# A recurrent attention kernel whose groups are brought one stage closer together, with three transposes moved to another engine

## The chip, the cores and the metric

One core of one Trainium2 chip. Times are device microseconds of one execution.

## The reference

```python
for t in range(S):                              # q, k, v, alpha: (4, 8, 768, 48)
    state = alpha[:, :, t, :, None] * state + einsum('bhd,bhe->bhde', k[:, :, t], v[:, :, t])
    y[:, :, t] = einsum('bhd,bhde->bhe', q[:, :, t], state)
x = y.transpose(0, 2, 1, 3).reshape(B, S, H * D)          # (4, 768, 384)
proj = x @ w_in                                           # 384 -> 1024
val, gate = proj[..., :512], proj[..., 512:]
for t in range(S):
    h = exp(A_log)[0] * h + val[:, t]                     # a[0, 0], as the reference has it
    ys[:, t] = h
out = (silu(gate) * ys) @ w_out                           # 512 -> 384
```

`w_in` and `w_out` come as float64 and are converted on the chip, in 12 units.

## The kernel before

The sequence is cut into N = 12 groups of 256 steps (4 batches of NG = 3 groups). A group goes through three stages, each a generator that the schedule steps: `front` (q, k and alpha are turned so that channels lie on the partitions; the running products V and P of alpha are scanned; Q = q·P, K = k·V; scores; keys turned back), `back` (states, values, eviction to `x_sb`, and `features`, which turns `x_sb` into `xT`), and `ssm` (four chunks of 6 matmuls, each chunk followed by a scan `hh`, a SiLU and a product `f`; then two output halves). In the profiles each of these matmuls counts as two instructions, so a chunk is 12 there (576 `pj` for 12 groups of four chunks). Each engine runs its instructions in the order in which the schedule issues them, as the profiles show: in the kernel before, the transposes for K end on TensorE at 210.13 us (209.09 + 1.04), but VectorE, which has `f` ahead of K, waits 0.45 us for the SiLU, starts `f` at 210.43 and K at 210.77.

```python
def load_heads(dst, src, n, queue=nc.sync):
    b, g = divmod(n, NG)
    for c in range(G):
        rows = ds(g * GC + c * C, C)
        queue.dma_start(out=dst[:, c, :, 0:D], in_=src[b, :, rows, :].rearrange("h p d -> p h d"))

def ssm(n, xT, prev_h, pool, ps_mm):
    ...
    for cc in range(NI):
        pj = ps_mm.tile([C, 2, GC], FP32, tag="mm", name="pj")
        ...                                      # 6 matmuls of w_in against xT (12 in the trace)
        nc.vector.tensor_tensor_scan(out=hh, ...)
        nc.scalar.activation(sg, pj[:, 1, :], AF.Silu)
        nc.vector.tensor_mul(f[:, cc, :], sg, hh)
        yield
    for c in range(G):
        ...                                      # output half: 4 matmuls of w_out (8 in the trace), eviction, store
        yield

def features(x_sb, xT, ps_tp):
    for c in range(G):
        ...                                      # 3 transposes on TensorE
        nc.scalar.activation(xT[:, :, ds(c * C, C)], tp, AF.Copy)

def front(n):
    ...
    def turned(name, jj):                        # 4 transposes on TensorE into PSUM (2 buffers)
        ...
    for jj in range(NP // 2):
        tp = turned("a", jj)
        ...                                      # scans V, reciprocal, scans P
    yield
    ...                                          # Q from turned("q", jj) and P; yield
    ...                                          # K from turned("k", jj) and V; yield
    ...                                          # scores, masked; yield
    keys_back(K, Kn, ps_tp)
    yield

for n in range(N + 3):                           # turn n: front(n), back(n-1), ssm(n-2), outputs of n-3
    ...
```

So a group's `xT` is finished in one turn and multiplied by `w_in` only in the next. While the weights are still being converted (turns 0 to 2), the conversion of units is placed between the steps.

## Time and profile before

| kernel | median us | range | profiled span | TensorE busy | VectorE busy |
|---|---|---|---|---|---|
| before | 347.33 (4 runs) | 346.2 to 348.6 | 344.2 | 309.7 | 198.6 |

The time of a run exceeds its own span (first to last instruction of the profile) by 1.6 to 2.3 us; the profiled run of this kernel took 345.98 us.

Cut at 98.1 us, where its steady turns have begun, and at the end of the turn of group 11 (295.9 us), this kernel is a start of 98.1, eight turns of together 197.8 (TensorE busy for 197.8), and an ending of 48.3 us.

### The profile page before, as it was taken

How to read it: one execution, taken by the hardware profiler on the slowest of the kernel's cores; microseconds unless marked ns; L12 is line 12 of the kernel's file. 1: busy time of each engine (PE TensorE's matmuls, PEld its weight loads, DVE VectorE, ACT ScalarE, POOL GpSimd, SP SyncE). 2: the span in 40 equal slices, each digit the busy share in tenths (PEclk: the TensorE clock that was granted, in tenths of full speed). 3: DMA queues.
4: the chain of work that ended last, by engine and by line, in shares of the span. 5: the costliest groups of instructions: out<-in, count | busy, mean ns of one | idle time of the engine just before them, and what ended most of it. 6: DMA issues, size and time to landing. Idle time of an engine off the chain costs nothing.

```text
span 344.2 us, 9637 instructions
## 1 busy us (share of the span) xinstructions
PE 309.7 (90%) x4233; PEld 249.6 (73%) x4233; DVE 198.6 (58%) x374; ACT 126.5 (37%) x267; POOL 32.3 (9%) x54
## 2 busy tenths in 40 slices
PE   2556696879999999999999999999999999997994
PEld 1345585757877878868868878878878878776772
DVE  2869797683566566475484494484475574314140
ACT  1356876743324324324333342333233233222111
POOL 4023652440000000000000000000000000000000
PEclk9996798989999999999999999999999999999998
DMA  9999998504704907608609409519110010010101
GB/s 129 216 218 256 238 199 125 94 2 103 130 2 97 135 2 130 104 0 146 88 1 160 73 2 170 62 38 170 29 46 4 0 48 2 2 49 0 50 0 54
DMA packets 107650, 29.02 MB, mean 84 GB/s; under 512 B 100944, under 2 KB 107088, under 8 KB 107600
## 3 DMA queue, kind: packets, MB, share of 16 engines
q1 hardware_dynamic: 104992, 27.93, 46.4%
q10 hardware_dynamic: 2608, 0.40, 1.0%
q8 instruction: 35, 0.57, 0.7%
q14 instruction: 15, 0.12, 0.1%
HBM read 23.60 MB, written 4.72 MB: 82 GB/s over the span
## 4 chain that ended last, share of the span: by engine, by line
PE 80%; DVE 8%; ACT 5%; DMA 3%; issue 2%; SPq 1%; ACTq 0%; DVEq 0%
PE pj L93 36%; PE o L107 18%; PE tp L295 9%; PE z L131 3%; PE sc L332 3%; PE y L146 3%; PE y L164 3%; PE tpk L119 3%; PE tpx L173 2%; DVE V L302 2%; DVE P L307 2%; DMA a_pad<-in_alpha_dram 2%; DMA v_sb<-in_v_dram 1%; ACT ex L242 1%; ACT ex L241 1%
## 5 line engine op out<-in xcount | busy, mean ns | idle before, releaser
L93 PE MATMUL pj<-xT,w_in 128*128 128x256 f32 x576 | 135.2, 386 | 2.9 <-ACT sg L101 2.9
L93 PEld LDWEIGHTS pj<-xT,w_in 128*128 128x128 f32 x576 | 107.1, 192 | 17.5 <-POOL w_out L250 3.0
L107 PE MATMUL o<-w_out,f 128*128 128x384 f32 x192 | 65.9, 496 | 0.1
L96 DVE TENSOR_TENSOR_SCAN hh<-a_dec,hh,pj 128x256 f32<-128x256 f32 x32 | 23.9, 747 | 69.0 <-PE pj L93 69.0
L101 ACT ACTIVATE sg<-pj 128x256 f32<-128x256 f32 x48 | 18.4, 383 | 114.1 <-DVE hh L96 114.0
L107 PEld LDWEIGHTS o<-w_out,f 128*128 128x128 f32 x192 | 35.9, 192 | 23.7 <-DVE f L102 0.7
L102 DVE TENSOR_TENSOR f<-sg,hh 128x256 f32<-128x256 f32 x48 | 20.9, 436 | 25.4 <-ACT sg L101 25.4
L302 DVE TENSOR_TENSOR_SCAN V<-tp,bias 128x256 f32<-128x256 f32 x48 | 30.1, 669 | 6.9 <-PE tp L295 6.9
L307 DVE TENSOR_TENSOR_SCAN P<-tp,iV,bias 128x256 f32<-128x256 f32 x48 | 33.4, 737 | 0.8
L312 ACT ACTIVATE junk<-V,bias 128x1024 f32<-128x1024 f32 x12 | 13.8, 1148 | 47.2 <-DVE V L302 47.2
L295 PE MATMUL tp<-ident,a_pad 128*128 128x128 f32 x96 | 13.9, 289 | 14.0 <-POOL k_pad L201 4.9
L96 DVE TENSOR_TENSOR_SCAN hh<-a_dec,pj 128x256 f32<-128x256 f32 x16 | 11.0, 685 | 23.8 <-PE pj L93 23.8
L295 PEld LDWEIGHTS tp<-ident,a_pad 128*128 128x128 f32 x96 | 11.6, 147 | 15.9 <-POOL k_pad L201 4.9
L349 POOL TENSOR_TENSOR S_n<-S_end,V 128x192 f32<-128x192 f32 x7 | 3.6, 513 | 203.5 <-DVE S_end L358 203.5
L295 PE MATMUL tp<-ident,q_pad 128*128 128x128 f32 x96 | 14.4, 292 | 8.0 <-DVE P L307 6.4
L295 PEld LDWEIGHTS tp<-ident,q_pad 128*128 128x128 f32 x96 | 11.9, 151 | 12.2 <-issue 8.6
L335 DVE COPY_PREDICATED A<-mask,sc 128x512 f32<-128x512 uint8 x24 | 16.0, 720 | 3.0 <-PE sc L332 3.0
L319 DVE TENSOR_TENSOR Q<-tp,P 128x512 f32<-128x512 f32 x24 | 15.4, 681 | 2.9 <-PE tp L295 2.9
L332 PEld LDWEIGHTS sc<-Q,K 64*64 64x64 f32 x768 | 13.7, 143 | 4.0 <-issue 3.0
L110 ACT ACTIVATE o_sb<-o 128x384 f32<-128x384 f32 x24 | 10.7, 479 | 15.5 <-PE o L107 15.5
L323 DVE TENSOR_TENSOR K<-tp,V 128x512 f32<-128x512 f32 x24 | 15.5, 681 | 0.5 <-PE tp L295 0.5
L332 PE MATMUL sc<-Q,K 64*64 64x64 f32 x768 | 15.5, 231 | 0.1
(61 smaller groups left out, 313.8 us busy)
## 6 DMA issues: line engine op xcount, KB each, us to landing
a_pad<-in_alpha_dram SPq DMA_DIRECT2D x24, 192.0 KB, 4.7
k_pad<-in_k_dram SPq DMA_DIRECT2D x24, 192.0 KB, 5.2
v_sb<-in_v_dram SPq DMA_DIRECT2D x24, 192.0 KB, 5.1
out_dram<-o_sb SPq DMA_DIRECT2D x24, 192.0 KB, 2.2
q_pad<-in_q_dram SPq DMA_DIRECT2D x22, 192.0 KB, 4.9
bits<-in_moe_w_in_dram SPq DMA_DIRECT2D x8, 384.0 KB, 5.3
bits<-in_moe_w_out_dram SPq DMA_DIRECT2D x4, 384.0 KB, 5.1
q_pad<-in_q_dram ACTq DMA_DIRECT2D x2, 192.0 KB, 5.5
```

The costliest lines, as they stand in the source:

```text
L93: nc.tensor.matmul(pj[:, i, :], w_in[:, kk, i, ds(cc * C, C)], xT[:, kk, :], start=(kk == 0), stop=(kk == NK - 1))
L96: nc.vector.tensor_tensor_scan(out=hh, data0=a_dec[:, cc:cc + 1].to_broadcast([C, GC]), data1=pj[:, 0, :], initial=prev_h[cc][:, GC - 1:GC ...
L101: nc.scalar.activation(sg, pj[:, 1, :], AF.Silu)
L102: nc.vector.tensor_mul(f[:, cc, :], sg, hh)
L107: nc.tensor.matmul(o, f[:, cc, ds(c * C, C)], w_out[:, cc, :], start=(cc == 0), stop=(cc == NI - 1))
L295: nc.tensor.transpose(tp[:, u, ds(c * C, C)], pad[name][:, c, 2 * j:2 * j + 2, :], ident)
L302: nc.vector.tensor_tensor_scan(out=V[:, 2 * jj + u, GC - 1::-1], data0=tp[:, u, ::-1], data1=bias[:, 1:2].to_broadcast([C, GC]), initial=1 ...
L307: nc.vector.tensor_tensor_scan(out=P[:, 2 * jj + u, :], data0=tp[:, u, :], data1=bias[:, 1:2].to_broadcast([C, GC]), initial=iV0[:, 2 * jj ...
L319: nc.vector.tensor_mul(Q[:, js], turned("q", jj), P[:, js])
L323: nc.vector.tensor_mul(K[:, js], turned("k", jj), V[:, js, 1:GC + 1])
L332: nc.tensor.matmul(scv[ds(R * r, R), i, c * NP + j, :], K[rows, j, steps], Q[rows, j, steps], start=True, stop=True, skip_group_check=True)
L335: nc.vector.copy_predicated(out=A[:, i].rearrange("p x t -> p (x t)"), mask=mask[:, ds(i * GP * R, GP * R)], data=sc[:, i])
```

## The change

Intent: a group's SSM block follows it one turn sooner (group n - 1 instead of n - 2), and from the fifth group on the q, k and alpha transposes are VectorE's, so TensorE gets 24 transposes less in each of eight groups. The loads of these groups place blocks of 32x32 for VectorE's transpose (`W = 32` in the kernel); they come in batches of a whole sequence, in packets of 128 and 64 bytes. Conversion of a unit is cut in two (U: split, J: join) and placed inside the first SSM blocks. The schedule becomes a string per turn: F a step of front(n), A of front(n+1), B of back(n), S of ssm(n-1), O an output of n-2, L and M loads.

```diff
+        BY_VECTOR = NG + 1
+        def load_batch(b):
+            ...
+                for j, nj in [(0, NP)] if w0 == 0 else [(j, 1) for j in range(NP)]:
+                    for i in range(2):
+                        for half in range(2):
+                            ...
+                            nc.sync.dma_start(out=tv[ds(DP * i + W * half, W), ...], in_=src[...])
         def front(n):
+            def squares(name, dst):
+                nc.vector.transpose(dst, batches[b, name][:, :, ds(g * GC, GC)])
+            if by_vector:
+                squares("a", aT)
             for jj in range(NP // 2):
-                tp = turned("a", jj)
+                tp = aT[:, js] if by_vector else turned("a", jj)
                 ...                              # scans V, P of half jj
+                yield
+            if by_vector:
+                squares("q", Q)
-                nc.vector.tensor_mul(Q[:, js], turned("q", jj), P[:, js])
+                nc.vector.tensor_mul(Q[:, js], Q[:, js] if by_vector else turned("q", jj), P[:, js])
             ...                                  # the same for k, K, V
-            nc.sync.dma_start(out=out[...], in_=o_sb)
+            nc.scalar.dma_start(out=out[...], in_=o_sb)
-        places = {0: (0, 0, 0, 1, 1), 1: (1, 1, 1, 1, 2), 2: (1, 1, 1, 1, 1)}
+        early = ["FFFFLUFUJFBJBBB", "FUUSJJFUUSJJFUUSJJFLSFFBUBJUBJB", "FUSJUFJSFFFFOBBSABASABOM"]
+        usual = "FLSSFFOABBSABASBOM"
+        ending = ["SSOSOS", "OO"]
-            for n in range(N + 3):
+            for n in range(N + 2):
                 ...
```

(Cut: heads are paired differently, tiles share memory, buffers of Q, K, A, Kn and x_sb are one fewer, the fallback path follows suit.)

## The prediction

> **What bounds the kernel now.** I read the page's busy times and its strip of 40 slices first, then the busy time by stretches (one per turn), then the groups, then the three timelines of one steady turn.
>
> ```profile
> PE 309.7 (90%) x4233; PEld 249.6 (73%) x4233; DVE 198.6 (58%) x374; ACT 126.5 (37%) x267; POOL 32.3 (9%) x54
> PE   2556696879999999999999999999999999997994
> DMA  9999998504704907608609409519110010010101
> ...
> 0.00:20.00 20.00, 8.98 (x96) 6.82 (x96) 11.00 (x18) 4.53 (x7) 4.04 (x23) 1.00 1.27 171
> 20.00:45.00 25.00, 15.07 (x339) 12.87 (x342) 21.34 (x43) 19.86 (x40) 12.46 (x12) 0.80 1.10 252
> 45.00:73.00 28.00, 21.24 (x311) 17.64 (x306) 21.68 (x44) 19.39 (x39) 11.58 (x13) 0.93 0.77 107
> 98.10:122.83 24.73, 24.73 (x344) 20.16 (x343) 15.10 (x28) 8.26 (x18) 0.52 (x1) 1.00 0.49 82
> ```
>
> The reader sees two kernels in one. From 73 us on a turn takes 24.73 us and TensorE is busy for all of it; nothing else is near full (VectorE 15.1). Nine such turns (groups 3 to 11) run from 73 to 296 us, then some 48 us of last SSM work. Before 73 us TensorE is idle for about 28 us, at a granted clock down to 0.80, and VectorE (21.3 of 25) and ScalarE (19.9 of 25) carry the load: this is where the weights are converted.
>
> ```profile
> L295 PE MATMUL tp<-ident,a_pad 128*128 128x128 f32 x96 | 13.9, 289 | 14.0 <-POOL k_pad L201 4.9 <-ACT Kn L120 4.1 <-issue 3.1
> L101 ACT ACTIVATE sg<-pj 128x256 f32<-128x256 f32 x48 | 18.4, 383 | 114.1 <-DVE hh L96 114.0
> L102 DVE TENSOR_TENSOR f<-sg,hh 128x256 f32<-128x256 f32 x48 | 20.9, 436 | 25.4 <-ACT sg L101 25.4
> ...
> 206.39 2.86 PE L93 MATMUL pj<-xT,w_in 128*128 128x256 f32 x12
> 209.29 0.69 DVE L96 TENSOR_TENSOR_SCAN hh<-a_dec,pj 128x256 f32<-128x256 f32 x1 [2.16 <-PE pj L93]
> 210.01 0.39 ACT L101 ACTIVATE sg<-pj 128x256 f32<-128x256 f32 x1 [3.31 <-DVE hh L96]
> 210.43 0.43 DVE L102 TENSOR_TENSOR f<-sg,hh 128x256 f32<-128x256 f32 x1 [0.45 <-ACT sg L101]
> 210.77 1.28 DVE L323 TENSOR_TENSOR K<-tp,V 128x512 f32<-128x512 f32 x2
> ...
> 206.77 2.28 SPq L83 DMA_DIRECT2D a_pad<-in_alpha_dram  x2
> ```
>
> These lines give the latency of an SSM chunk: hh starts 0.2 us after the last of its 12 matmuls, the SiLU waits for hh, f waits for the SiLU; from the start of hh to the next VectorE instruction is 1.48 us, 0.45 of it idle. VectorE and ScalarE run in program order, so each such wait also holds all behind it. The last line shows that the issue of two 1024-packet loads holds its queue for 2.28 us.
>
> [...] 104992 packets took 46.4% of 16 engines' 344.2 us, 24 ns each, though most hold only 192 B. [...]
>
> **Part 1, transposes off TensorE.** In the steady turn the q, k and alpha transposes hold TensorE 0.96 + 0.97 + 0.96 = 2.9 us (from start to start of the next group, for example 105.41 to 106.37). Eight of twelve groups lose them: 23 us of TensorE work gone, and a TensorE-bound turn would be 24.7 - 2.9 = 21.9 us. VectorE gains three transposes[...]: V/P scans 5.6, hh 2.8, f 1.4, A 1.3, states 1.5, Q and K 2.6[...], SiLU waits 1.8, in all 20.4 of 21.9 us. That fits only if nothing waits.
>
> **Part 2, the new turn's loop.** The stages are now one turn closer, so I followed the program order with measured durations, from the start of the last hh of a turn (t = 0). SiLU ends at 1.1. ScalarE then evicts xT (0.87), because features come after that chunk in its order: 2.0. TensorE's next chunk needs this xT: start 2.2. From there TensorE is full: two chunks 5.3, scores 1.1, key transposes 0.9, half an output 2.6, states 1.1, values 1.1, third chunk 2.7, to 17.0. Then hh, SiLU, f 0.2 + 1.5, V/P scans of the next group's second half 2.8, [...]Q multiply 1.3, and the last hh can start: 23.9 us. In that time TensorE has 21.9 us of work; the 2.0 us between are idle after the last output. So I expect about 23.9 us a turn, 0.8 less than now, not 2.9. ScalarE now also issues two v loads and two output stores, before the junk pair (2.5 us) and the first SiLU. Up to about 1.4 us per load this is hidden by the wait for the second chunk; at 2.4 us, as in a crowded queue, the turn becomes about 26.
>
> **Part 3, the start.** Converting one unit costs ScalarE 2.2, VectorE 0.7 + 0.5, GpSimd 2.0 us. Six w_in units now stand inside the first SSM block: each chunk needs the two units before it joined, and its SiLU stands behind the ScalarE work of the two units after. From f to f: two joins 1.0, V/P 2.8, first mask 0.35, ScalarE 1.75 + 0.55 + 1.75, SiLU and f 0.85: 9.0 us. The other two chunks go through join, GpSimd 3, matmuls 2.9, hh to f 1.5: 8.5. Group 0 passes front and back alone, about 34 us until its xT (alpha lands at 7.5; the old trace has K at 17.8, and conversions, Kn, states, values and evictions add 16). First f 8.7 later, three more chunks 26, then A to xT of group 1 11.5: 80 us. The next turn (two groups' V/P, one SSM block, VectorE-bound with ScalarE's waits) adds 32: the turn of group 3 starts at 112, or 115 with matmuls at the lowered clock[...] in the old trace. The old kernel is at the like point (SSM of group 1 multiplied) at 98. So the shorter pipeline does not shorten the start; I expect it to lose some 15 us there.
>
> **Sum.** Start 115 + eight turns with a following group 8 x 23.9 = 191 + turn of group 11, TensorE-bound, 21.9 + last SSM block and outputs 16.1 + 5.3 + flag and f waits 3.5 + tail 4.8 = 357.6 us of span. Run time is 347.34 - 344.2 = 3.1 us above the span: 361. This charges every wait I can see. If half of the start's loss is absent (106) and the turn is 22.7 us, the same sum gives 106 + 181.6 + 51.6 + 3.1 = 342. Hand chains of this length tend to double-count, and such a carefully arranged schedule was presumably meant to gain, so I take the middle, **350 us**.
>
> **Rivals.** (a) TensorE stays the bound: turn 21.9, start as good as before in useful work (103): 103 + 175.2 + 51.6 + 3.1 = 333 us. For it: 20.4 of 21.9 us on VectorE does fit. Against it: the loop from hh through SiLU, xT and the next chunk has no slack. (b) ScalarE's issues hold the first SiLU: 25 to 26 us a turn, 8 x 1.5 more, some 370 us. For it: 2.3 to 4.8 us per pair of loads in the SP rows; against: only while the queue is crowded. (c) The loads bind. 8 groups x 3 tensors x 2048 more packets = 49152, at 20 to 24 ns over 16 engines 61 to 74 us more transfer time, on 160 us in a span of 350: room on average, but a batch of three groups takes some 46 us. It is asked for two turns ahead, so I think it is hidden; late by one tensor it costs 5 to 15 us once.
>
> **Range and chances.** 334 to 364 us: from rival (a) to the full sum. Faster by over 2% (below 340.4) needs both a good start and a TensorE-bound turn: 0.25. Within 2%: 0.43. Slower (above 354.3): 0.32.
>
> **What would show it.** Steps are right if steady turns measure 23 to 25 us with TensorE idle 1 to 3 us, ended by the xT eviction or a SiLU, while VectorE is above 80% busy; if the first steady turn starts after 108 us[...]. Wrong if turns are 22 us without idle TensorE[...], if the start is over by 100, or if TensorE waits for the new batch loads.

Cut, where marked, are reasons, with the duration of a VectorE transpose: an estimate that no trace had shown, as the kernel before has no such instruction. The sums still contain it: three such terms in the 20.4 us of VectorE a turn, one in the loop's 23.9 us, and so eight in 191, in the 357.6 us of span and in the 361 us of time. The terms that can still be read come to 17.0 and 22.8 us. The 24 ns per packet is the profile page's average; from 80 to 93 us the same trace has 19.4 ns (8605 packets, 80.3% of 16 engines' 13 us).

## More of the kernel before

Beside the lines that the prediction shows, one more matters, the chain of work that ended last, followed back from the last instruction, as shares of the span by engine:

```profile
PE 80%; DVE 8%; ACT 5%; DMA 3%; issue 2%; SPq 1%; ACTq 0%; DVEq 0%
```

TensorE (PE) is four fifths of the chain.

## The result, and the profile after

The changed kernel takes **364.6 us** (4 runs, 363.01 to 365.35), against 347.33 before: ratio 1.049 [1.044, 1.054], slower.

Busy times, the strip of TensorE in 40 slices, and the chain by engine, from the page of the changed kernel:

```profile
PE 296.5 (82%) x4041; PEld 232.3 (64%) x4041; DVE 230.8 (64%) x397; ACT 127.2 (35%) x267; POOL 57.3 (16%) x72
...
PE   2558276684895997998998989979989799799993
...
PE 57%; DVE 24%; ACT 8%; DMA 4%; issue 3%; POOL 1%; SPq 1%; DVEq 0%; POOLq 0%; ACTq 0%
```

TensorE is busy for 13 us less (not 23: the group of `pj` matmuls alone, the same 576, takes 141.7 us instead of 135.2, part of them at a lower clock: the mean granted over the span is 0.941, against 0.973) and for a smaller share of a longer span: after the start its slices now read 7, 8 and 9, where the old kernel had a row of nines. In the chain VectorE's share has gone from 8% to 24%. The same, by stretches (columns: length; busy time of TensorE, its weight loads, VectorE, ScalarE, GpSimd, each with its count; granted clock; DMA share; GB/s). The stretches are the turns of groups 1 and 2, then two steady turns:

```profile
32.69:77.28 44.59, 26.86 (x344) 21.54 (x344) 26.83 (x53) 24.96 (x50) 17.00 (x16) 0.81 0.46 99
77.28:119.56 42.28, 32.25 (x379) 25.74 (x379) 25.73 (x46) 12.31 (x26) 12.70 (x11) 0.85 0.28 39
...
192.80:216.81 24.01, 22.03 (x318) 17.26 (x318) 19.37 (x32) 8.16 (x19) 0.51 (x1) 1.00 1.14 116
264.46:288.48 24.02, 22.04 (x319) 17.27 (x319) 18.98 (x32) 8.17 (x19) 0.51 (x1) 1.00 0.15 35
```

Cut in three like the old kernel:

| | start | eight turns | ending | span |
|---|---|---|---|---|
| before | 98.10 | 197.80 | 48.30 | 344.2 |
| after | 119.56 | 192.79 | 48.55 | 360.9 |
| difference | +21.46 | -5.01 | +0.25 | +16.7 |

The eight turns gained 5 us, not the 23 us that the removed transposes had held TensorE; the start lost 21. (The start ends where the turn of group 4 begins in the old kernel and that of group 3 in the changed one, with the SSM of group 1 multiplied in both. The two do not stand at exactly the same instruction, so this is an accounting, not yet an explanation.)

The chain in one steady turn, in order of time (start, us, what), shows why it takes 24 us:

```profile
190.91 0.67 DVE hh L105
...
191.88 0.88 ACT xT L183 x2
...
192.80 5.45 PE pj L102 x24
...
204.96 2.80 PE pj L102 x12
...
207.78 0.76 DVE hh L105
...
209.41 1.20 DVE V L338 x2
...
210.82 1.64 DVE P L343 x2
212.46 1.15 DVE Q L329
...
213.63 1.29 DVE Q L352 x2
214.92 0.67 DVE hh L105
...
215.89 0.88 ACT xT L183 x2
...
216.81 1.35 PE pj L102 x5
```

It is a closed loop: from the `hh` of one turn's last chunk (190.91) through the xT eviction and TensorE's work to the next turn's (214.92), 24.01 us. The old chain at this place is TensorE alone. VectorE's leg in it, 207.78 to 214.92, is scans, the new q transpose (L329, 1.15) and a multiply, all of them ahead of `hh` in VectorE's order. TensorE's wait at the seam, from the view of waits (total, times, longest):

```profile
PE pj L102 <- ACT xT L183: 14.6, 8, 2.0
PE pj L102 <- POOL w_in L288: 12.4, 4, 6.8
PE tp L325 <- DVE P L343: 7.8, 3, 4.0
```

The first line is the loop: eight waits, 1.8 us each. The other two are the start: chunks that wait for converted weights, and TensorE transposes that wait for a scan to free one of the two PSUM buffers they write into.

### The profile page after: what moved, and what is told of

Its sections match the earlier page's. It is cut to its first block, busy times and chain, and to the rows that moved or that the text cites. A ratio compares the mean times of both kernels' runs of the same rounds, so it can differ in the third digit from the quotient of the medians.

```text
span 360.9 us, 9309 instructions
## 1 busy us (share of the span) xinstructions
PE 296.5 (82%) x4041; PEld 232.3 (64%) x4041; DVE 230.8 (64%) x397; ACT 127.2 (35%) x267; POOL 57.3 (16%) x72
## 4 chain that ended last, share of the span: by engine, by line
PE 57%; DVE 24%; ACT 8%; DMA 4%; issue 3%; POOL 1%; SPq 1%; DVEq 0%; POOLq 0%; ACTq 0%
PE pj L102 28%; PE o L116 12%; DVE P L343 5%; DVE V L338 5%; DVE hh L105 4%; PE sc L372 4%; PE z L140 3%; DVE Q L352 3%; PE tpk L128 3%; PE y L155 3%; DVE Q L329 3%; PE tp L325 2%; ACT xT L183 2%; DMA batch<-in_k_dram 2%; ACT sg L110 2%
## 5 line engine op out<-in xcount | busy, mean ns | idle before, releaser
L102 PE MATMUL pj<-xT,w_in 128*128 128x256 f32 x576 | 141.7, 401 | 27.0 <-ACT xT L183 14.6
L110 ACT ACTIVATE sg<-pj 128x256 f32<-128x256 f32 x48 | 18.2, 380 | 115.6 <-DVE hh L105 115.5
L325 PE MATMUL tp<-ident,pads 128*128 128x128 f32 x96 | 18.5, 339 | 19.5 <-DVE P L343 7.8
L228 POOL MEMSET batch<- 32x1536 f32 x18 | 24.7, 1371 | 53.3 <-DMA batch<-in_q_dram 31.8
L325 PEld LDWEIGHTS tp<-ident,pads 128*128 128x128 f32 x96 | 14.1, 172 | 23.5 <-issue 14.5
L343 DVE TENSOR_TENSOR_SCAN P<-aT,iV,bias 128x256 f32<-128x256 f32 x32 | 23.4, 773 | 0.6
L338 DVE TENSOR_TENSOR_SCAN V<-aT,bias 128x256 f32<-128x256 f32 x32 | 20.6, 685 | 0.3
L360 ACT ACTIVATE junk<-V,bias 128x1024 uint8<-128x1024 f32 x12 | 13.8, 1147 | 18.3 <-issue 14.1
L338 DVE TENSOR_TENSOR_SCAN V<-tp,bias 128x256 f32<-128x256 f32 x16 | 10.1, 672 | 15.7 <-PE tp L325 15.7
L140 PE MATMUL z<-v_sb,Kn 64*64 64x48 f32 x768 | 13.8, 220 | 4.5 <-ACT Kn L129 4.5
L173 PEld LDWEIGHTS y<-S_n,Q 64*64 64x64 f32 x704 | 13.1, 140 | 6.4 <-ACT fence L160 3.3
L173 PE MATMUL y<-S_n,Q 64*64 64x48 f32 x704 | 14.6, 227 | 3.0 <-ACT fence L160 3.0
```

Source lines behind the costliest of these rows:

```text
L102: nc.tensor.matmul(pj[:, i, :], w_in[:, kk, i, ds(cc * C, C)], xT[:, kk, :], start=(kk == 0), stop=(kk == NK - 1))
L140: nc.tensor.matmul(zv[chs, r, g, j, :], Kn[rows, g, j, chs], v_sb[rows, g, NP * i + j, :], start=True, stop=True, skip_group_check=True)
L173: nc.tensor.matmul(yv[at, i, c, j, :], Q[rows, j, ds(R * x, R)], S_n[rows, x, j, :], start=False, stop=(c == G - 1 and j == NP - 1), skip_ ...
L228: nc.gpsimd.memset(tv[ds(DP * i + W, W), :, D - W:W], 1.0 if name == "a" else 0.0)
L325: nc.tensor.transpose(tp[:, u, ds(c * C, C)], pad[name][:, c, j], ident)
L338: nc.vector.tensor_tensor_scan(out=V[:, 2 * jj + u, GC - 1::-1], data0=tp[:, u, ::-1], data1=bias[:, 1:2].to_broadcast([C, GC]), initial=1 ...
```

## The experiments

Each is an edit of the changed kernel unless said otherwise; "before" ran in the same rounds. All results were correct but one, which is named.

### 1. e1_swap: the last SSM chunk before the next group's q

```diff
-        usual = "FLSSFFOABBSABASBOM"
+        usual = "FLSSFFOABBSABSBAOM"
```

The same instructions; only the last S and B (SSM chunk, features) now stand before the A that holds the q transpose and Q.

> Edit: in the steady turn the last SSM chunk's scan, SiLU and product stand ahead of the next group's q transpose and Q multiply, instead of behind them. Theory (the loop hh, SiLU, xT, two chunks ... third chunk, V/P, q transpose, Q, hh sets the turn): the loop loses 2.4 us and drops to 21.5, below TensorE's 21.9 to 22.0 us of work, so the turns of groups 3 to 10 go from 23.8 to 24.0 to about 22.0, TensorE no longer waits for xT, and the run goes from 364 to about 349 us. Rival (ScalarE's v loads, stores and junk pair hold the first SiLU): the turn stays within 0.3 us of 23.9, the run above 361. Rival (VectorE is simply full): the turn stays too, as no VectorE work is taken away.

Measured: 345.77 us (344.85 to 347.53), ratio to before 0.9996 [0.9956, 1.0036]; span 342.7, so 18.2 us under the changed kernel's. The first two of its eight turns take 22.6 and 22.2 us, the other six 21.8; all eight 175.41 (119.34 to 294.75), against 192.79. Two of the six by stretches:

```profile
185.88:207.64 21.76, 21.76 (x319) 17.36 (x318) 18.63 (x32) 8.28 (x18) 0.51 (x1) 1.00 1.15 121
207.64:229.42 21.78, 21.78 (x335) 17.37 (x334) 18.70 (x32) 8.48 (x18) 0.51 (x1) 1.00 1.14 118
```

TensorE is busy for all of a turn of 21.8 us, with VectorE's load what it was (18.6 us) and the DMA share the same 1.15. So the 2 us a turn came from the place of the q work in VectorE's order, not from VectorE's total or the batch loads. This kernel, 3 us better than expected, only equals the old one because its start (119.34) is still as long as the changed kernel's.

### 2. e2_start: the first SSM block joins its units in another order

```diff
-  early[1] = "FUUSJJFUUSJJFUUSJJFLSFFBUBJUBJB"
+  early[1] = "UUFJJSUUFJJSUUFJJSFLSFFBBBBUUJJ"
```

The two units of a chunk are joined one step sooner, ahead of the scan and SiLU of the chunk before; two w_out units go to the end of the turn.

> Edit: only the order of the turn of group 1. The two units of a chunk are masked before that turn's V/P, joined before the chunk's scan, and the two w_out units come after the back part of group 1. Theory (the start is slow because each chunk waits for its units through VectorE's order, ScalarE and GpSimd, one after the other): from chunk to chunk 6.7 us instead of 8.5 to 9, and the first value fence no longer behind a unit's ScalarE work; the turn of group 1 ends 6 to 10 us earlier than 77.3 us, steady turns unchanged at 23.9, run about 356 us. Rival (the start is limited by the arrival of the weights over the DMA queues): the turn ends at the same time, run 363 or more.

Measured: 358.09 us (356.07 to 359.5), ratio 1.0329 [1.0275, 1.0383], span 356.0. The turn of group 2 starts at 67.53 instead of 77.28, 9.8 us sooner, but steady turns begin at 114.48 instead of 119.56: half is given back in the turn of group 2. TensorE's timeline there (start, busy, and in brackets the wait before and what ended it):

```profile
82.87 1.09 PE L325 MATMUL tp<-ident,pads 128*128 128x128 f32 x4 [7.37 <-DVE P L343]
```

In the changed kernel the like transposes wait 3.99 us. The two joins at the end of the turn now stand in VectorE's order ahead of the next scans of V and P, and wait there for ScalarE's part of the conversion (5.01 and 1.45 us); TensorE's transposes wait for the scans. So in this part of the start the wait is handed on through VectorE's order; TensorE's work does not set it.

### 3. e4_old_vec: the new loads and VectorE's transposes in the old order

The old three-stage schedule, written as strings, with VectorE's transposes from the fifth group on (and the buffers that this order needs).

```diff
-  early, usual, ending = (as changed)
+  early = ["FFFFLFCFC", "FFCBFCBFLCBFBCFCC", "FFCBSSFCBSFLCBSFBCFCM", "FFBTOOFBSFLBSFABSFSM"]
+  usual = "FBOOFFLBSBSFABSFSM"      # B is back(n-1), S is ssm(n-2), T loads the first batch
```

> Edit: the change's loads, head pairs and VectorE transposes are kept, but the order of work is that of the kernel before (three stages, conversions where they were), with the first half of the next group's V/P moved into the turn before. Theory (the transposes are worth TensorE's 2.9 us a turn as soon as the turn has slack, and the new start is what cost): start as in the kernel before (turn of group 4 starts near 98 us), eight turns of 21.9 to 22.5 us, run about 324 us (322 to 330). Rival (VectorE with 20 us a turn, or the batch loads, holds the turn near 24): run 338 or more.

Measured: 344.95 us (344.39 to 347.02), ratio 0.995 [0.9916, 0.9984]. The expectation was missed by 21 us. In the old order the first batch of VectorE loads is needed sooner, and it came too late (its rival, 338 us or more, had named the batch loads). The issuing queue (SyncE's: start, time, what, count), then VectorE at the transpose of group 4's k:

```profile
74.97 12.57 SPq L233 DMA_DIRECT2D batch<-in_alpha_dram  x16
87.58 19.03 SPq L233 DMA_DIRECT2D batch<-in_q_dram  x16
106.65 9.99 SPq L233 DMA_DIRECT2D batch<-in_k_dram  x16
```

```profile
119.02 1.25 DVE L330 STREAM_TRANSPOSE K<-batch 128x1024 f32<-128x1024 f32 x1 [7.42 <-DMA batch<-in_k_dram]
```

From the start of the first to the end of the last of the 48 issues 41.7 us pass, but SyncE issues for only 25.6 of them. Asked what the queue itself waited for, the view of waits has this, between 74 and 125 us (total, times, longest):

```profile
SPq L233 <- DMA v_sb<-in_v_dram: 9.9, 1, 9.9
```

That is a load of v on ScalarE's queue, issued there only at 101.98: the next q transfer of the batch waits until it has landed, while no DMA engine moves anything from 98.4 to 102. Waits for output stores take 4.2 us more, and in the second batch waits for v loads take 20.0. As k came 7.4 us late, the wait for the v load alone would account for it; no run takes it away. Group 4's turn is 32.5 us long (101.23 to 133.72, from one group of state matmuls to the next), group 6's 26.0; the others settle at 22.85. These two turns are some 13 of the 21 us. In the changed kernel the queue has such waits too (36 us in the two batches), but there 53 us lie between the first transfer and the moment when VectorE wants k, here 37. So the batch is hidden in the changed kernel because it gives it more time, which the prediction's rival (c) had asked about; in the old order it is not.

### 4. e5_tensor and e5b_tensor: the new order, all transposes on TensorE

```diff
-        BY_VECTOR = NG + 1
+        BY_VECTOR = N               # and q, k, alpha loaded each turn instead of in batches
```

> Edit: the changed kernel with all groups turned by TensorE, so only the new order of work and its smaller parts are left of the change. Theory: TensorE-bound turns of 24.8 us after the slow start, so the run is 7 us slower than the changed kernel, about 371 us: the VectorE transposes brought 0.9 us a turn there, not 2.9. Rival (VectorE's transposes are what slows the changed kernel): this run is at or under 364.

This run gave a wrong result (389.86 us): the load of group 4's q, k and alpha was left out by mistake, so it is not used; its expectation of 371 fails with the mended run as well. Mended, with an expectation that was read off e5's own trace:

> Edit: e5 mended (the loads of q, k and alpha of group 4 had been left out, so its result was wrong). Theory, after e5's trace: in the new order TensorE's transposes of the next group stand between the matmuls, and with two PSUM buffers the second half waits for the V/P scans, so VectorE's latency enters TensorE's order: turns of 27 us, run about 388 us. Rival (the missing loads made e5 slow): turns of 24.8, run about 371.

Measured: 387.86 us (387.05 to 388.94), ratio 1.1182 [1.1121, 1.1243]. A steady turn takes 27.06 us (200.94 to 228.00). From the view of waits and from TensorE's timeline in such a turn:

```profile
PE tp L325 <- DVE P L343: 27.5, 11, 3.7
```

```profile
220.83 0.63 PE L325 MATMUL tp<-ident,pads 128*128 128x128 f32 x4 [2.53 <-DVE P L343]
```

In the new order TensorE's q transposes stand behind scans of the same turn, and the wait is 2.5 us. So in the new order the move to VectorE is worth 3 us a turn (27.06 to 24.01), about what the three transposes had held TensorE; the idle time that remains is not the same wait: 2.5 us before the q transposes there, 1.8 us for xT here. It is the order that is dear: the same 4233 TensorE instructions take a span of 346.8 us in the old order (the next run) and 385.9 in the new.

### 5. e6_old_tensor: the old order, all transposes on TensorE, with the change's small parts

The paired heads, the smaller loads, v loads and stores on ScalarE's queue and the 8-bit junk output, in the old order (which again needs the old number of buffers of Q, K, A, Kn and x_sb, and the old placing of the conversions).

```diff
-        BY_VECTOR = NG + 1
+        BY_VECTOR = N
-  early, usual, ending = (as changed)
+  early = ["FFFFLFCFC", "FFCBFCBFLCBFBCFCC", "FFCBSSFCBSFLCBSFBCFCM"]; usual = "FFBOOFBSFLBSFBSFSM"
```

> Edit: the changed kernel's smaller parts (head pairs, pair loads in more DMAs, v and output DMAs on ScalarE's queue, one-byte junk) with TensorE's transposes for all groups and the order of work of the kernel before. Theory: these parts are nearly free, turns of 24.7 us, start 2 us later: 346 to 350 us. Rival (ScalarE's DMA issues cost as much as the loop): turns of 25.5 or more, run 354 or more.

Measured: 349.23 us (348.29 to 350.51), ratio 1.0073 [1.0014, 1.0131]. The small parts cost 0.7%, not 5%. What costs is the order.

### 6. e7_start_swap: both cures together

```diff
-  early = ["FFFFLUFUJFBJBBB", "FUUSJJFUUSJJFUUSJJFLSFFBUBJUBJB", "FUSJUFJSFFFFOBBSABASABOM"]
-  usual = "FLSSFFOABBSABASBOM"
+  early = ["FFFFLUFUJFBJBBB", "UUFJJSUUFJJSUUFJJSFLSFFBBBBUU", "FJJSUUFSJJFFFFOBBSABSBAOAM", "SFLSFFOABBSABSBAOM"]
+  usual = "FLSSFFOABBSABSBAOM"
```

The joins of the w_out units are spread into the turn of group 2 between scans; the loop is cut as in e1.

> Edit: e1 and a start rearranged further: e2's turn of group 1, the joins of the last units after the next scans, and in the turn of group 2 the SSM chunk, the features and an output ahead of the next group's second V/P half and Q. Theory (order, not work, makes the start slow): the first steady turn starts 8 to 12 us before e1's 119, turns 21.8, run 334 to 338 us. Rival (the start is full of work): it stays above 115 us, run above 342.

Measured: **331.24 us** (329.41 to 331.77), ratio 0.9537 [0.9478, 0.9595]: better than expected, 4.6% under the kernel before, and by the two ratios (0.9537 / 1.049) some 9% under the changed one. The turn of group 2 begins at 66.3, steady turns at 104.33. From there to 300 us, by stretches:

```profile
104.33:300.00 195.67, 195.38 (x2962) 155.87 (x2961) 157.06 (x262) 73.67 (x159) 19.53 (x18) 1.00 0.62 78
```

TensorE is idle for 0.3 us in 196, so the removed transposes are collected in full, and the start is now only 6 us behind the old kernel's 98.1. Nothing but the order of instructions separates this kernel from the changed one.

### 7. e8_old_7th and e9_old_7th_later: the old order, VectorE from the seventh group on

With later VectorE groups the first batch has time in the old order too. Both runs also have the key transposes ahead of the last two chunks. The runs differ in one letter's place: T asks for the batch before the last pad loads of the TensorE groups, or after.

```diff
-  "FFBTOOFBSFLBSFBSFSM"       # e8: turn of group 3
+  "FFBOOFBSFLTBSFBSFSM"       # e9
```

> Edit: e4 with VectorE's transposes only from the seventh group on, so that no batch is wanted before it can have arrived, and key transposes ahead of the last two chunks. Theory (e4 lost 11 us in the turn of group 4 and 5 after it to batches that landed late, and 0.7 a turn to Kn behind a SiLU): start as before, three turns of 24.8, six of 21.9: about 346 + 2 - 6 x 2.8 = 331 us. Rival (VectorE is too full for 21.9): turns of 22.8 and more, run above 337.

> Edit: e8 with its first batch asked for after the last pad loads instead of before them, as in e8 TensorE waited 7 us each in two turns for pads that stood behind the batch in the SP queue. Theory (the transposes are worth 2.1 to 2.9 us a turn in the old order once nothing waits for a load): the two waits go, turns of 22.6, run 330 to 334 us. Rival (packets of batch and pads share the engines anyway): over 340.

Measured: e8 345.93 us (345.12 to 346.58), ratio 0.9963 [0.991, 1.0017], well over its expectation. SyncE's queue, then TensorE:

```profile
104.84 11.21 SPq L233 DMA_DIRECT2D batch<-in_k_dram  x4
116.15 14.51 SPq L91 DMA_DIRECT2D pads<-in_alpha_dram  x4
```

```profile
133.19 1.73 PE L326 MATMUL tp<-ident,pads 128*128 128x128 f32 x7 [7.27 <-DMA pads<-in_alpha_dram]
```

The pads that are needed next stand behind the batch that is needed in three turns, and TensorE waits 7.3 us for them. But the four pad loads do not need 14.5 us to be issued (the next four take 2.1). Of that time SyncE itself waits, by the view of waits between 116 and 131 us:

```profile
SPq L91 <- DMA v_sb<-in_v_dram: 10.3, 1, 10.3
```

It is again a v load on ScalarE's queue (issued at 126.71), not the batch's packets. That the batch put the pads where this wait falls is argued from what comes next: with the letter moved, SyncE has no wait for a v load between 80 and 140 us, and e9 takes 336.95 us (336.77 to 337.22), ratio 0.9725 [0.9696, 0.9755], somewhat over its expectation; its VectorE turns take 22.60 us, TensorE busy 22.35. So VectorE's transposes pay in the old order too, 2.1 us of a turn in the six groups that have them (24.73 to 22.60). The transposes were not the harm; the place of one of them in the order was.

### 8. e10_more_on and e11_more_off: one more transpose on the loop, and off it

The loop is said to run through the q transpose and not through the alpha transpose. Each run does one of them twice.

```diff
 e10             if by_vector:
                     squares("q", Q)
+                    squares("q", Q)
 e11             if by_vector:
                     squares("a", aT)
+                    squares("a", aT)
```

> Edit: the changed kernel with the q transpose done twice, 1.24 us more of VectorE in each of eight turns, between the V/P scans and the last chunk's scan, so on the loop. Theory (that loop sets the turn): turns grow by all of it, 23.9 to 25.1 us, run 10 us longer, about 374. Rival (the last chunk's scan is not what the next turn waits for): under 368.

> Edit: the changed kernel with the alpha transpose done twice, the same 1.24 us of VectorE, but ahead of the V/P scans of the first half, where VectorE waits 1.15 us for the third chunk later in the turn. Theory: nearly all of it goes into that wait, turns 23.9 to 24.2, run 0 to 3 us longer than 364. Rival (VectorE's load as such sets the turn): as much longer as with the q transpose, about 374.

Measured: e11 365.64 us (365.1 to 367.75), ratio 1.0572 [1.0525, 1.0619]: 1 us over the changed kernel's median, within what was expected for 9.9 us more VectorE work. e10 382.14 us (381.45 to 384.95), ratio 1.105 [1.0992, 1.1108]: 17.5 over it, where 8 x 1.24 = 10 was expected. TensorE at the seam of e10, in two turns:

```profile
224.36 7.13 PE L102 MATMUL pj<-xT,w_in 128*128 128x256 f32 x24 [3.26 <-ACT xT L183]
...
278.33 5.45 PE L102 MATMUL pj<-xT,w_in 128*128 128x256 f32 x24 [3.01 <-ACT xT L183]
```

The wait for xT grew from 1.8 to some 3.1 us, as the loop says. In six of the eight turns the 24 matmuls after it then took 7.13 instead of 5.45 us (in one of eight in the changed kernel), in turns with a mean granted clock of 0.94 instead of 1.00 (the last section shows when). That accounts for the excess in the profiled span, 380.4 against 360.9: the waits for xT are 24.9 us in all against 14.6, which is 10.3; five more slow pairs of chunks are 5 x 1.68 = 8.4; the start is 1.0 longer. The place of the work in the order decided, not its amount.

## Why the prediction was right or wrong

It was wrong in its number: 364.6 us against 350, with a range that ended at 364 and a chance of 0.32 for slower. Its mechanism held; by its own steps:

- **Transposes off TensorE, 2.9 us a turn.** Right. With the loop cut (e1) six turns are 21.8 us against 21.9 predicted, TensorE-bound; the eight are 22.4 shorter than the old kernel's (197.80 - 175.41), against 23 predicted.
- **The loop, 23.9 us a turn.** Right, and shown by e1, e10 and e11. From `hh` to `hh` 24.01; the next chunk starts 1.89 us after `hh` (2.2 predicted), the third chunk ends at 16.85 (17.0), SiLU and f done 1.65 later (1.7), V and P 3.05 (2.8), q transpose 1.17 (its term is cut), Q multiply 1.29 (1.3). Eight turns were to take 191 and took 192.8. The sum let each turn be equal; one of them (143.69 to 169.03) took 25.34 because its first two chunks took 7.13 us, at a lowered clock.
- **VectorE's 20.4 us a turn.** Its busy time is 18 to 19.4: the 1.8 us of SiLU waits were counted with the work and are idle in the trace (and four `f` of 436 ns are 1.7 us, not 1.4). So the sign "VectorE above 80% busy" failed, 149.0 of 192.8 us being 77%; the signs of turn, idle time and start came true, but for the one turn of 25.34. The duration that the sum had for a transpose (cut) was the author's estimate; measured, 1.22 to 1.24 us. Nothing hangs on these.
- **ScalarE's issues, rival (b).** Refuted: turns are 24.0 us both where loads crowd the queue (DMA share 1.14) and where they do not (0.15).
- **The batch loads, rival (c).** Refuted for this order (VectorE waited 0.6 us in all for them), though e4 shows that with less lead they would have cost half a turn. Of the 61 to 74 us more of transfer time that it reckoned, 31 came (53.9% of 360.9 us on the two queues against 47.4% of 344.2). **Rival (a)**, TensorE stays the bound, is what e1 and e7 built and the change did not.
- **The start.** The turn of group 1 was to end at 80 and ended at 77.28. The turn of group 2 was to take 32, or 35 at the lowered clock, and took 42.3: start 119.56 against 115. Mis-sized, and not VectorE-bound as it was said to be (VectorE busy for 25.7 of 42.3 us): TensorE's transposes for two groups wait for VectorE's scans and a Q multiply (4.0, 2.2 and 2.2 us in the timeline) through the two PSUM buffers, which the sum did not have, at a granted clock of 0.85. e2 and e7 show that order alone moves this start by 5 and 15 us. No run isolates the two buffers from the clock.
- **The sum, 357.6 us of span.** 119.56 + 192.79 + 21.99 (turn of group 11, 21.9 predicted) + 26.56 (the rest, 29.7 predicted) = 360.9: 1% over. The sum plus 3.1, 361 us, is within 1% of the measured 364.6. That is partly luck: the start was 4.6 us too short and the rest 3.1 too long. The 3.1 itself sets the median of some runs against the span of another; that profiled run took 345.98, so the term is 1.8, and 2.1 for the changed kernel.
- **The step that failed:** "Hand chains of this length tend to double-count, and such a carefully arranged schedule was presumably meant to gain, so I take the middle, 350 us". Nothing in the profile spoke for it. The low case that went into the middle had a start of 106 and turns of 22.7; they measured 119.56 and 24.1 (192.79 / 8). Nor did the runs show 11 us of double counting: the turns and the turn of group 11 measured within 1% of their terms, the start 4% over, and only the rest lay under its term, by 3 us. The loop is exactly as long as its legs. That a change was meant to gain is no measurement; the gain on TensorE was real (22.4 us in e1), but 17.4 of it (192.79 - 175.41) was given back in the loop, and the start lost 21.5 us more. With 361 kept, the chance of slower by over 2% would have followed.

## What to carry to other kernels

When stages are moved closer together, walk one steady turn in each engine's program order from a late result back to itself: if that loop is longer than the bound engine's work, it sets the turn, whatever the busy shares say (here 24.0 us against TensorE's 22.0, with VectorE busy for 77%), and moving one block past another in the order (here two letters of a string, 18 us) can take it away. If such a walk is made from measured durations and its waits are really in program order, keep its sum; do not discount it because it is long or because the change was meant well. Ask of a queue's order as of an engine's: what is needed next goes ahead of what is needed in three turns (from e8 to e9, 345.93 to 336.95 us). Then ask what the queue itself waited for: in e4 and e8 it stood still, for 9.9 and 10.3 us, for a load that another engine was late to issue.

## What was measured besides

- The duration of a float32 transpose of 128x1024 on VectorE, 24 of them in the changed kernel (the 8 of k take 1240 ns each):

```profile
L329 DVE STREAM_TRANSPOSE aT<-batch 128x1024 f32<-128x1024 f32 x8 | 9.9, 1233 | 0.0
L329 DVE STREAM_TRANSPOSE Q<-batch 128x1024 f32<-128x1024 f32 x8 | 9.7, 1215 | 0.0
```

- When the granted clock fell. In the traces of the kernels before and after it is 1.00 or 0.50, and from its first record (18.14 and 17.94 us) to its last change (342.41 and 359.27 us) every stretch of one value lasts a whole multiple of 3.41 us. It falls 4 times before and 8 times after, each time at the end of such a step of 3.41 us in which TensorE was busy for 0.00 to 1.45 us; steps at 1.00 with 1.46 us (before, from 315.10) or more are followed by no fall. So a step that was idle in part was enough. In the changed kernel's steady turns the clock falls once, for 3.41 us at 144.23, just after the wait of 1.96 us before 143.69 (its profile by stretches, columns as above):

```profile
140.82:144.23 3.41, 1.45 (x6) 0.68 (x5) 2.96 (x5) 1.53 (x4) 0.00 (x0) 1.00 1.16 53
144.23:147.65 3.42, 3.42 (x10) 2.70 (x9) 1.62 (x3) 1.62 (x3) 0.00 (x0) 0.50 0.67 157
```

  In the stretch before the fall TensorE was busy for 1.45 of 3.41 us. The wait of 1.98 us before 216.81 was followed by no fall: counted on in steps of 3.41 us, a boundary (215.91) cuts it in two, and TensorE was busy for 2.34 and 2.52 us of the two stretches. In e10 the clock fell after a stretch with 1.03 us (it ended at 146.73) and stayed after one with 1.51 (it ended at 279.84). Half of 3.41 us is the 1.7 us by which a pair of chunks is longer (7.13 against 5.45). So in these runs the place of a wait against the steps decided with its length. The limit is not measured more closely than by these stretches, and busy time is as the profile models it.
- In e4 a transfer of the first batch takes 0.49 us to issue (median) and 2.5 us to land. Against that, a queue stood still for a transfer of another queue for 9.9 us in e4 and for 10.3 us in e8, for which TensorE waited 7.3 us.
